# Stacked attention items: every transposition takes 128 rows, and columns of zeros are overwritten within the unit

## The chip, the cores and the metric

The kernel runs on one core of one Trainium2 chip. The metric is the device time of one execution in microseconds (us), the median of several runs. A run is also profiled once; the profile's span is the time from the first to the last instruction of the program on that core.

## The reference

Causal attention in blocks of 64 positions, then two dense stages. All data is float32.

```python
batch, n_heads, seq, head_dim = (4, 8, 576, 64)
scores = scale * np.matmul(q, k.transpose(0, 1, 3, 2))
mask = block_i >= block_j                    # blocks of 64
attn = softmax(where(mask, scores, -1e9))
x = np.matmul(attn, v)                       # as 2304 rows of 512
h = np.maximum(np.maximum(x @ w1, x @ w2), x @ w3);  x = h @ w_out     # 512 -> 768 -> 512
h = x @ w_in;  g = h * np.cos(h);  out = g @ moe2_w_out                # 512 -> 2048 -> 512
```

## The kernel before

Attention is cut into 32 items: batch (4), half of the rows (queries 0 to 319 and 320 to 575), pair of heads (4). An item goes through loads, `prep` (float32 split into two parts for the matrix products), `scores` (products into PSUM tiles SA and SB, row maximum on VectorE, exponential on ScalarE into the SBUF tiles `prob`, then each row is divided by its sum), `transposes` (TensorE turns 128 by 128 pieces of `prob` into the PSUM tile `tb`, and a copy by ScalarE or VectorE, `pt<-tb`, brings them to the SBUF tile `pt`), and `pv` (products of `pt` with the values, into the PSUM tile X). The matrix products of the first dense stage (tile `psm`) are put between the steps of the items as filling work; the second dense stage (`psm<-yh,w_in` and `po`) follows after the last item.

Items of batches 1 to 3 in the second half of the rows are "stacked" (line 572: `it.stacked = b > 0 and half == 1`); there are 3 x 4 = 12 of them. In a stacked item each 128-row tile of `prob` holds two blocks of 64 queries, and for each of its two heads (`e`) there are two tiles, a (448 columns used, `prob[6]` or `prob[7]`) and b (576 columns used, `prob[8]` or `prob[5]`). The causal mask makes the first 64 rows of a zero in its fourth piece of 128 columns (piece 3, counted from 0), and the first 64 rows of b zero in its fifth (piece 4). `transposes_stacked` therefore works in two units for each head. Unit h = 0 takes pieces 0 and 1 of a and b: four transpositions of 128 rows. Unit h = 1 takes piece 2 of a and b, piece 3 of a from row 64 on, piece 3 of b, and piece 4 of b from row 64 on: five transpositions, of which two take only the last 64 rows (written `64*128` in the profile: 64 rows, 128 columns loaded; the result has 64 columns). Both units fill one 512-column tile `tb`, which is then copied in one piece.

The order of all work is made by a planner (`Plan`). Calls to an engine are recorded as operations with a price and dependencies; those in a `with R.unit():` block are one operation. The planner then schedules all operations by list scheduling and emits the instructions of each engine in that order, so that each engine has a fixed queue. A transposition has a fixed price, whatever its size (`price`):

```python
if method == "transpose":
    return 109.0, late, False
```

For tiles in PSUM the planner takes the whole buffer as read or written, and for tiles in SBUF a range of columns of all rows. All calls pass through one helper line, so every instruction of the profile bears the same line number, L214, and is told apart by its tiles.

Of the kernel before, what the change touches and what calls it, by code (L numbers as in the profile page):

```python
# [19 lines left out]
P = 128  # L20
# [437 lines left out]
def fused_kernel(tc, qk, k1, v2, w1, w2, w3, wout, w_in2, w_out2, out):  # L458
# [11 lines left out]
    R = Plan(tc)  # L470
# [10 lines left out]
    ident = const.tile([P, P], F32, "ident")  # L481
# [191 lines left out]
    def transposes_stacked(it):  # L673
        it.pt = at.tile([P, 16 * P], F32, "pt", tag="pt")
        for e in range(2):
            a, b = (prob[where[e]] for *_, where in PAIRS)
            for h in range(2):
                tiles = [(a, 2 * h, 0), (b, 2 * h, 0)] + (
                    [(a, 1, 0), (b, 1, 0)] if h == 0 else [(a, 3, 64), (b, 3, 0), (b, 4, 64)])
                t = ps_x.tile([P, 512], F32, "tb", tag="T", bufs=2)  # L680
                with R.unit():
                    c0 = 0
                    for p, j, r in tiles:
                        R.tensor.transpose(t[:, c0:c0 + P - r], p[r:P, j * P:j * P + P], ident[r:P, r:P])
                        c0 += P - r
                c = 1024 * e + 512 * h
                R.copy(it.pt[:, c:c + 512], t)

# [57 lines left out]
    def transposes(it):  # L746
        if it.stacked:
            return transposes_stacked(it)
        order = it.f.order
        it.pt = at.tile([P, 16, P], F32, "pt", tag="pt")  # L750
        for c in range(0, len(order), 4):
            part = order[c:c + 4]
            n = P * len(part)
            t = ps_x.tile([P, 512], F32, "tb", tag="T", bufs=2)
            with R.unit():
                for x, (j, b) in enumerate(part):
                    R.tensor.transpose(t[:, x * P:x * P + P], prob[b][:, j * P:j * P + P], ident)
            R.copy(it.pt[:, c:c + len(part)].rearrange("p b n -> p (b n)"), t[:, :n])
# [349 lines left out]
```

## Time and profile before

| | us |
|---|---|
| runs: median of 3 (lowest, highest) | 893.09 (893.08, 893.38) |
| the profiled execution: its own time | 892.99 |
| the profiled execution: span of the core | 891.2 |
| TensorE matmul busy | 876.3 (98% of the span) |
| TensorE weight load busy | 720.7 (81%) |
| VectorE busy | 556.1 (62%) |
| ScalarE busy | 450.7 (51%) |

In the profile PE is a matmul and PEld the load of its weights, that is of the operand that stays in the array; for a transposition that is the piece of `prob`, and the identity streams past it. A matmul's duration includes its way through the array, so that the durations of neighbours overlap; what a matmul costs the queue is the distance from its start to the start of the next. DVE is VectorE, ACT is ScalarE, POOL is GpSimd, SP is SyncE. Between the span and the execution's own time lie 1.8 us.

### The profile page before, as it was taken

Reading aid. Unit: us, or ns where it says so; the run is one execution under the profiler, and the core shown is the slowest. Engines: PE = TensorE matmul, PEld = TensorE weight load, DVE = VectorE, ACT = ScalarE, POOL = GpSimd, SP = SyncE. Lnnn points to the kernel's source line nnn. Section 1 sums busy time; section 2 is a strip of 40 time slices with the busy share of each in tenths; the row PEclk is TensorE's granted clock in tenths of the full one; section 3 lists DMA queues with packets and bytes.
Section 4 is the critical chain, followed back from the end, with each engine's and each line's share of the span. In section 5 each row is a group of like instructions: output and inputs, shape, how many; then the busy total and the mean of one; then the engine's idle time right before and its main releaser. Section 6 shows DMA issues by size and latency. Waiting matters only on the chain.

```text
span 891.2 us, 12524 instructions
## 1 busy us (share of the span) xinstructions
PE 876.3 (98%) x4616; PEld 720.7 (81%) x4616; DVE 556.1 (62%) x1099; ACT 450.7 (51%) x974; POOL 6.5 (1%) x38
## 2 busy tenths in 40 slices
PE   7799999999999999999999999999999999999998
PEld 5577887888877888787789888888888888888897
DVE  6999987875566425534549797655464455455454
ACT  7997777775677515644555543332233223322333
POOL 0000000000000000000000000000000000000000
PEclk9999999999999999999999999999999999999999
DMA  7664637763346303511165851110001000100000
GB/s 258 227 206 148 187 119 232 246 192 120 94 140 232 113 1 125 201 61 54 64 205 180 331 190 48 48 48 1 0 25 48 1 0 1 48 1 0 24 24 24
DMA packets 43548, 95.05 MB, mean 107 GB/s; under 512 B 5856, under 2 KB 15072, under 8 KB 43488
## 3 DMA queue, kind: packets, MB, share of 16 engines
q1 hardware_dynamic: 43488, 94.26, 32.3%
q8 instruction: 36, 0.59, 0.3%
q14 instruction: 24, 0.20, 0.1%
HBM read 73.79 MB, written 20.45 MB: 106 GB/s over the span
## 4 chain that ended last, share of the span: by engine, by line
PE 95%; ACT 2%; DMA 1%; DVE 1%; issue 0%; SPq 0%; ACTq 0%; DVEq 0%
PE psm L214 56%; PE po L214 22%; PE tb L214 6%; PE X L214 5%; PE SA L214 3%; PE SB L214 3%; DMA raw<-w 1%; ACT prob L214 1%; ACT pt L214 0%; SPq L214 0%; DVE t L214 0%; DVE top L214 0%; ACT add L214 0%; DVE prob L214 0%; ACT t L214 0%
## 5 line engine op out<-in xcount | busy, mean ns | idle before, releaser
L214 PE MATMUL psm<-yh,w_in 128*128 128x512 f32 (+1 forms) x640 | 194.3, 368 | 0.0
L214 PE MATMUL po<-w_out,gh 128*128 128x512 f32 x576 | 177.6, 390 | 0.0
L214 ACT ACTIVATE th<-th,halfpi 128x512 f32<-128x512 f32 (+1 forms) x80 | 54.5, 682 | 189.1 <-DVE th L214 189.0
L214 PE MATMUL psm<-xhi,whi 128*128 128x512 f32 (+1 forms) x360 | 137.2, 381 | 0.0
L214 PEld LDWEIGHTS psm<-yh,w_in 128*128 128x128 f32 x640 | 117.0, 188 | 20.6
L214 PE MATMUL psm<-xlo,whi 128*128 128x512 f32 (+1 forms) x360 | 132.9, 369 | 0.0
L214 PE MATMUL psm<-xhi,wlo 128*128 128x512 f32 (+1 forms) x360 | 132.8, 369 | 0.0
L214 PEld LDWEIGHTS po<-w_out,gh 128*128 128x128 f32 x576 | 107.1, 188 | 21.2
L214 PE MATMUL psm<-yl,w_in 128*128 128x512 f32 (+1 forms) x320 | 117.7, 368 | 0.0
L214 PE MATMUL po<-w_out,gl 128*128 128x512 f32 x288 | 112.0, 389 | 0.0
L214 DVE TENSOR_SCALAR th<-psm 128x512 int32<-128x512 f32 (+1 forms) x80 | 50.9, 637 | 71.8 <-PE psm L214 71.7
L214 DVE TENSOR_TENSOR th<-psm,th 128x512 f32<-128x512 f32 (+1 forms) x80 | 50.9, 637 | 53.7 <-ACT th L214 53.7
L214 DVE TENSOR_TENSOR hm<-psm,hm 128x512 f32<-128x512 f32 (+1 forms) x60 | 38.1, 636 | 66.4 <-PE psm L214 65.6
L214 PEld LDWEIGHTS psm<-xhi,wlo 128*128 128x128 f32 x360 | 67.9, 189 | 11.8
L214 PEld LDWEIGHTS psm<-xhi,whi 128*128 128x128 f32 x360 | 67.9, 189 | 11.0
L214 PEld LDWEIGHTS psm<-xlo,whi 128*128 128x128 f32 x360 | 68.0, 189 | 9.1
L214 DVE TENSOR_TENSOR gl<-th,gh 128x512 fp32r<-128x512 f32 (+1 forms) x80 | 50.9, 636 | 38.3 <-ACT gh L214 38.3
L214 ACT CAST gh<-th 128x512 fp32r<-128x512 f32 (+1 forms) x76 | 43.9, 578 | 55.6 <-DVE th L214 55.6
L214 PE MATMUL tb<-ident,prob 128*128 128x128 f32 (+1 forms) x424 | 68.4, 278 | 3.4 <-ACT pt L214 2.9
L214 PEld LDWEIGHTS psm<-yl,w_in 128*128 128x128 f32 x320 | 60.3, 188 | 10.6
L214 ACT COPY pt<-tb 128x512 f32<-128x512 f32 (+1 forms) x101 | 55.9, 568 | 23.6 <-PE tb L214 23.1
L214 PEld LDWEIGHTS tb<-ident,prob 128*128 128x128 f32 (+1 forms) x424 | 51.1, 140 | 20.3 <-issue 5.2
(104 smaller groups left out, 1311.2 us busy)
## 6 DMA issues: line engine op xcount, KB each, us to landing
raw<-w SPq DMA_DIRECT2D x18, 512.0 KB, 3.8
raw<-w_in SPq DMA_DIRECT2D x16, 512.0 KB, 3.7
raw<-w_out SPq DMA_DIRECT2D x16, 512.0 KB, 3.9
k<-k SPq DMA_DIRECT2D x24, 288.0 KB, 3.0
vr<-v SPq DMA_DIRECT2D x16, 320.0 KB, 3.2
kept_in<-both SPq DMA_DIRECT2D x10, 512.0 KB, 3.6
w_in<-kept_in SPq DMA_DIRECT2D x10, 512.0 KB, 9.7
out<-osb SPq DMA_DIRECT2D x18, 256.0 KB, 2.0
```

What stands on the lines that cost most here:

```text
L214: return lambda: getattr(real, method)(*[value(a) for a in args], **{k: value(a) for k, a in kw.items()})
```

## The change

In `transposes_stacked`, each piece now gets the column `c0` of `tb` at which it is written, and every transposition takes all 128 rows and writes 128 columns. Unit h = 0 keeps its pieces, their order and places. In unit h = 1 the pieces that took 64 rows now write their 64 columns of zeros first, to columns that a later transposition of the unit fills: piece 3 of a is written to columns 192 to 319, then piece 2 of a to 0 to 127 and piece 2 of b to 128 to 255 (over the zeros in 192 to 255); piece 4 of b is written to 384 to 511, then piece 3 of b to 320 to 447 (over the zeros in 384 to 447). What stands in `tb` at the end of the unit, and so the copy and all that follows, is as it was.

```diff
-                tiles = [(a, 2 * h, 0), (b, 2 * h, 0)] + (
-                    [(a, 1, 0), (b, 1, 0)] if h == 0 else [(a, 3, 64), (b, 3, 0), (b, 4, 64)])
+                tiles = [(a, 0, 0), (b, 0, P), (a, 1, 2 * P), (b, 1, 3 * P)] if h == 0 else [
+                    (a, 3, 192), (a, 2, 0), (b, 2, P), (b, 4, 384), (b, 3, 320)]
                 t = ps_x.tile([P, 512], F32, "tb", tag="T", bufs=2)
                 with R.unit():
-                    c0 = 0
-                    for p, j, r in tiles:
-                        R.tensor.transpose(t[:, c0:c0 + P - r], p[r:P, j * P:j * P + P], ident[r:P, r:P])
-                        c0 += P - r
+                    for p, j, c0 in tiles:
+                        R.tensor.transpose(t[:, c0:c0 + P], p[:, j * P:j * P + P], ident)
                 c = 1024 * e + 512 * h
                 R.copy(it.pt[:, c:c + 512], t)
```

## Rows read from the trace of the kernel before

**Rows 1.** First lines of the page: busy us (share of span) xinstructions.

```profile
span 891.2 us, 12524 instructions
PE 876.3 (98%) x4616; PEld 720.7 (81%) x4616; DVE 556.1 (62%) x1099; ACT 450.7 (51%) x974; POOL 6.5 (1%) x38
```

**Rows 2.** Busy time by stretch: length, engines' busy us (instructions), clock, DMA share, GB/s.

```profile
100.00:451.00 351.00, 351.00 (x1952) 281.98 (x1951) 207.15 (x428) 213.09 (x498) 5.08 (x24) 1.00 0.43 137
451.00:891.00 440.00, 436.58 (x2151) 370.74 (x2149) 258.74 (x445) 153.81 (x259) 0.00 (x0) 1.00 0.18 60
```

**Rows 3.** Waits of PE, 0 to 100 us, first and last: us, times, longest.

```profile
PE SB L214 <- ACT prob L214: 4.1, 4, 1.1
...
PE SB L214 <- ACT knat L214: 0.3, 1, 0.3
```

**Rows 4.** Groups by form, PE, 128 to 442: xcount | busy us, mean ns | idle.

```profile
L214 PE MATMUL tb<-ident,prob 128*128 128x128 f32 x240 | 39.7, 280 | 0.0
L214 PE MATMUL tb<-ident,prob 64*128 64x64 f32 x48 | 13.0, 271 | 0.0
```

**Rows 5.** Timeline of PE, both units: start, length, instruction (first of several merged).

```profile
253.88 0.39 PE L214 MATMUL psm<-hl,vhi 128*128 128x512 f32 x1
254.10 0.39 PE L214 MATMUL psm<-hh,vlo 128*128 128x512 f32 x1
254.34 0.60 PE L214 MATMUL tb<-ident,prob 128*128 128x128 f32 x4
...
255.71 1.05 PE L214 MATMUL tb<-ident,prob 128*128 128x128 f32 x5
256.68 0.50 PE L214 MATMUL psm<-hh,vhi 128*128 128x512 f32 x1
257.02 0.39 PE L214 MATMUL psm<-hl,vhi 128*128 128x512 f32 x1
```

**Rows 6.** Timeline of the weight loads, same unit of five.

```profile
255.58 0.27 PEld L214 LDWEIGHTS tb<-ident,prob 128*128 128x128 f32 x2
256.01 0.60 PEld L214 LDWEIGHTS tb<-ident,prob 64*128 64x128 f32 x3 [0.17 <-issue]
256.68 0.19 PEld L214 LDWEIGHTS psm<-hh,vhi 128*128 128x128 f32 x1
```

**Rows 7.** Timeline of PE where all transpositions have 128 rows.

```profile
217.15 0.60 PE L214 MATMUL tb<-ident,prob 128*128 128x128 f32 x4
...
217.81 0.40 PE L214 MATMUL psm<-xlo,whi 128*128 128x512 f32 x1
...
286.92 0.71 PE L214 MATMUL tb<-ident,prob 128*128 128x128 f32 x5
287.38 0.36 PE L214 MATMUL SA<-kh,qh 128*128 128x256 f32 x1
...
329.31 1.03 PE L214 MATMUL tb<-ident,prob 128*128 128x128 f32 x8
...
330.41 0.39 PE L214 MATMUL psm<-xlo,whi 128*128 128x512 f32 x1
```

**Rows 8.** Timeline of the weight loads of those eight.

```profile
329.07 1.03 PEld L214 LDWEIGHTS tb<-ident,prob 128*128 128x128 f32 x8
```

**Rows 9.** Timeline of PE: a run of nine (unit of four, then unit of five).

```profile
236.28 1.48 PE L214 MATMUL tb<-ident,prob 128*128 128x128 f32 x9
...
238.02 0.39 PE L214 MATMUL psm<-xlo,whi 128*128 128x512 f32 x1
```

**Rows 10.** Timeline of PE with scores (SA) as the neighbours.

```profile
373.14 0.60 PE L214 MATMUL tb<-ident,prob 128*128 128x128 f32 x4
...
373.70 0.29 PE L214 MATMUL SA<-kl,ql 128*128 128x288 f32 x1
373.84 1.05 PE L214 MATMUL tb<-ident,prob 128*128 128x128 f32 x5
...
375.05 0.29 PE L214 MATMUL SA<-kl,ql 128*128 128x288 f32 x1
```

**Rows 11.** Busy time, stretches with changed units: PE, PEld, DVE, ACT, POOL.

```profile
128.00:180.00 52.00, 52.00 (x326) 40.61 (x325) 39.85 (x86) 38.94 (x94) 0.00 (x0) 1.00 0.68 222
236.00:281.00 45.00, 45.00 (x273) 34.87 (x273) 27.52 (x55) 33.31 (x81) 0.00 (x0) 1.00 0.49 157
370.00:442.00 72.00, 72.00 (x379) 57.02 (x379) 31.53 (x56) 36.56 (x75) 0.00 (x0) 1.00 0.18 56
```

**Rows 12.** Timeline of DVE: last scaling of `prob` before a transposition.

```profile
249.66 0.51 DVE L214 TENSOR_SCALAR prob<-prob,sums 128x576 f32<-128x576 f32 x1
```

**Rows 13.** Timeline of PE at that place.

```profile
250.69 0.55 PE L214 MATMUL tb<-ident,prob 128*128 128x128 f32 x3
```

**Rows 14.** Waits of ACT and DVE, 128 to 180, longest totals: us, times, longest.

```profile
ACT pt L214 <- PE tb L214: 4.9, 8, 1.7
DVE top L214 <- PE SB L214: 5.6, 7, 1.6
DVE top L214 <- PE SA L214: 2.7, 3, 1.7
```

**Rows 15.** Timeline of ACT: copy after the unit of four of rows 5.

```profile
254.97 0.59 ACT L214 COPY pt<-tb 128x512 f32<-128x512 f32 x1 [1.12 <-PE tb L214]
```

## The prediction

> **What bounds the kernel now.** The page's busy line comes first: PE has 98% of the span, no other engine over 62% [rows 1]. An average does not say that PE sets the pace where the change is, so the table by stretch comes next: from 100 to 451 us PE is busy for all 351.00 of 351.00 us, at a granted clock of 1.00, while DVE and ACT are busy for 207 and 213 [rows 2]. Since busy PE time includes the way through the array, it alone does not rule out short waits, and the list of PE's waits is third: the stretch up to 100 us has seven rows, 11.2 us together, and the list of the whole span has the same seven, so none lies behind [rows 3]. The 48 transpositions of 64 rows all start between 128 and 442 us, with no idle PE time before any of them [rows 4]. So all that changes lies in a stretch where PE issues without a pause, and what a unit of transpositions gives up there goes to the end of the span one for one, unless another engine becomes late. Behind 451 us there are 2151 matmuls of PE, 436.58 us in 440.00, which also only follow earlier [rows 2].
>
> **What a unit costs now.** A matmul's length overlaps its neighbours, so a unit is read from starts: from its first transposition to the start of the second matmul behind it, since the first matmul behind it starts early and stays long (at 256.68 it lasts 0.50 us, its like 0.39 [rows 5]). A unit of five before `psm`: 255.71 to 257.02, 1.31 us [rows 5]. The same measure where all transpositions have 128 rows: four take 217.15 to 217.81, 0.66 us; eight take 329.31 to 330.41, 1.10 us [rows 7]. Four more cost 0.44, so one costs 0.11 us, and a unit of five would take 0.66 + 0.11 = 0.77. The excess of today's unit is 1.31 - 0.77 = 0.54 us. A run of nine (a unit of four, then one of five) confirms it: 236.28 to 238.02 is 1.74 us [rows 9], against 1.10 + 0.11 = 1.21, an excess of 0.53. With scores as the neighbours: 373.84 to 375.05 is 1.21, the unit of four ahead of it 373.14 to 373.70 is 0.56, plus 0.11 gives 0.67, an excess of 0.54 [rows 10]. It does not depend on what follows.
>
> Where the excess sits is seen in the weight loads. Eight loads of 128 rows run from 329.07 for 1.03 us without a gap, beside the matmuls, which start at 329.31 [rows 7, 8]: each load is done under the matmul ahead. In the unit of five the third load, the first of 64 rows, waits 0.17 us for nothing that the profile shows ("issue"), and the next matmul's load starts only at 256.68, with that matmul [rows 6]. I read this as the array running empty each time the height of the operand changes, four times in a unit: into and out of each of the two 64-row pieces.
>
> **The change part by part.** Removed: 48 transpositions of 64 rows, two in each of 12 items x 2 heads = 24 units [rows 4], and with them the four changes of height in each unit. Added: 48 transpositions of 128 rows in their place; five stay five. Each is twice as high and writes twice the columns. No row shows one that overwrites another's columns, so I bound it: below, nothing beyond the 0.11 us that a full transposition costs [rows 7]; above, by the wait in the third rival. I take the lower end, since the nearest row shows overwriting in flight: the `psm` matmuls of one group write the same 512 columns, start 0.22 us apart (253.88, 254.10) and last 0.39, so the second starts to write while the first is still under way, with no gap [rows 5]. Sum for a unit: 1.31 - 0.77, or 1.74 - 1.21; I take 0.53. 24 x 0.53 = 12.7 us.
>
> Moved: only the order inside units of h = 1. The first transposition there now reads the fourth piece of a. That calls for no later operation than before: one scaling instruction covers all used columns of a tile (128x576 in [rows 12]), and the unit h = 0 ahead of it already reads the same tiles. The planner's price of a transposition is 109 ns in either size, the recorded operations and the column ranges that it sees are the same, so I expect the same queues on every engine; no DMA is added or passed. Unit h = 0 issues the same instructions as before. The copy `pt<-tb` stays one of 512 columns, 0.59 us [rows 15]; it ends earlier with its unit.
>
> What could be late next: scaling of `prob`, which must end before the first transposition. At 250.69 it had ended at 249.66 + 0.51 = 250.17, 0.52 us earlier [rows 12, 13], and between that item's last scores and this place stands no changed unit, so both move together. Where a changed unit does lie between, PE arrives 0.53 us earlier and uses up such a margin, and might stand for a few tenths. I take nothing off for it in the forecast.
>
> Against the profiled execution: span 891.2 - 12.7 = 878.5, its own time 892.99 - 12.7 = 880.3. The median of the runs stands 0.10 above that execution: 893.09 - 12.7 = 880.4.
>
> **Rivals.** First, part of the gain is absorbed. Between 128 and 180 us lie 8 of the 24 units (16 transpositions of 64 rows), and DVE and ACT are busy for 39.85 and 38.94 of 52 us [rows 11]. If their chain set the pace there as soon as PE is faster, the 8 x 0.53 = 4.2 us of that stretch would be lost: 884.6. Against it: in that stretch ACT waits 4.9 us for `tb` and DVE 8.3 us for scores [rows 14], which an earlier PE gives back; from 236 to 281 and from 370 to 442, with 8 units each, the two engines have more room [rows 11]. 0.15, most of it for a loss of 1 to 2 us.
>
> Second, the change doesn't do what it says: the excess comes not from the height but from the place of those pieces, and stays. 893.1. Against it: the unit of five at 286.92, of 128 rows throughout, takes 0.46 us to the next matmul [rows 7], today's 0.97 [rows 5]. 0.03.
>
> Third, the other side: the overwriting transposition waits until the zeros under it are written. In a unit, piece 2 of b comes two transpositions (0.22 us) after piece 3 of a, and piece 3 of b one (0.11) after piece 4 of b. A transposition lasts 0.27 us [rows 4], a handover 0.03 (`tb` ends at 254.34 + 0.60 = 254.94, ACT starts at 254.97 [rows 5, 15]). If only the matmul waits, the two lose 0.30 - 0.22 = 0.08 and 0.30 - 0.11 = 0.19, together 0.27 of the 0.53: 893.09 - 24 x 0.26 = 886.9. If the wait also keeps back the weight load (0.27 for two, about 0.14 each [rows 6]), they lose 0.55: 24 x 0.02 slower, 893.6; and if each such wait also costs the 0.17 us of idle time that the height change shows [rows 6], 0.89: 24 x 0.36 = 8.6 slower, 901.7. It decides from 0.265 us for each overwriting transposition. Against it stands the row of `psm` above, and that one engine's queue is in order. 0.02 for 886.9, 0.03 for the slower end.
>
> Fourth, a mechanism of the weight loads: full-height loads wait for the matmul ahead, since both use the whole array, and only pieces of another height get in beside it. Each transposition of 128 rows would then cost 0.27 + 0.14 = 0.41 us, a unit of five 2.05 instead of 1.31: 24 x 0.74 = 17.8 slower, 910.9. The Trainium skill says so in TensorE: Matmul & The Clock Gate, Part 3 (What overlaps and what doesn't): a weight load runs beside a matmul only when their row groups differ. By that rule one would keep the 64-row pieces. The trace says otherwise: the eight full-height loads follow each other under running matmuls [rows 7, 8], and it is the 64-row load that stands [rows 6]. 0.01.
>
> **How the numbers follow.** Forecast 0.76: 880.4, by itself 879.6 (a unit saves 0.56, 0.02 of reading error in each) to 882. The range reaches to the whole price of the first rival, 884.6. Left out are 886.9 and beyond, 0.09 together. What a measurement of this kernel can tell from no change is about 0.2%, 1.8 us. Faster: 0.76 + 0.15 + 0.02 = 0.93; the same: 0.03; slower: 0.03 + 0.01 = 0.04.
>
> **What would show it.** In the changed kernel's profile: no form `64*128` under `tb`, 424 transpositions of 128 rows in all and 4616 matmuls; units of five that take 0.77 us to the second matmul before `psm`, runs of nine 1.21; weight loads in them without idle time by "issue"; PE's list of waits still empty behind 100 us. A gain below 12 us with units at 0.77 means new waits of PE, by name in that list, and points to the first rival; units near 1.04 or 1.31 and more point to overwriting (third) or to the place of the pieces (second). A changed order of the queues would make the argument from the planner wrong.

## The result, and the profile after

| | before | after |
|---|---|---|
| median of 4 runs (lowest, highest), us | 893.09 (893.02, 893.38) | 881.27 (880.12, 882.92) |
| ratio, 95% interval | | 0.9868 [0.9851, 0.9886] |
| the profiled execution: its own time; span | 892.99; 891.2 | 880.12; 878.3 |

The kernel became 11.8 us faster by the medians, 12.9 by the two profiled executions. The forecast was 880.4.

The first lines of the page after, as in [rows 1]:

```profile
span 878.3 us, 12524 instructions
PE 863.8 (98%) x4616; PEld 718.1 (82%) x4616; DVE 555.7 (63%) x1099; ACT 449.6 (51%) x974; POOL 6.5 (1%) x38
```

The number of instructions is the same on every engine, and in the traces every engine issues them in the same order, by their tiles, as the prediction expected of the planner. PE's busy time fell by 12.5 us; DVE and ACT have done the same work.

The forms under `tb`, on PE between 127 and 430 us (columns as in [rows 4]):

```profile
L214 PE MATMUL tb<-ident,prob 128*128 128x128 f32 x288 | 39.6, 274 | 0.0
```

240 + 48 = 288: the 64-row form is gone, the number is kept. Two units of the changed kernel on PE's timeline, four then five, answering [rows 5], the loads of the second, answering [rows 6], and a run of nine, answering [rows 9]:

```profile
248.28 0.60 PE L214 MATMUL tb<-ident,prob 128*128 128x128 f32 x4
...
249.66 0.71 PE L214 MATMUL tb<-ident,prob 128*128 128x128 f32 x5
250.12 0.48 PE L214 MATMUL psm<-hh,vhi 128*128 128x512 f32 x1
250.44 0.39 PE L214 MATMUL psm<-hl,vhi 128*128 128x512 f32 x1
```

```profile
249.53 0.60 PEld L214 LDWEIGHTS tb<-ident,prob 128*128 128x128 f32 x5
250.09 0.19 PEld L214 LDWEIGHTS psm<-hh,vhi 128*128 128x128 f32 x1
```

```profile
231.76 1.14 PE L214 MATMUL tb<-ident,prob 128*128 128x128 f32 x9
232.66 0.47 PE L214 MATMUL psm<-xhi,whi 128*128 128x512 f32 x1
232.98 0.39 PE L214 MATMUL psm<-xlo,whi 128*128 128x512 f32 x1
```

The five loads follow one another for 0.60 us with no idle time marked, and the load of the next matmul starts at 250.09, 0.03 before that matmul; the unit of [rows 6] had 0.17 of "issue" and behind it a load that started with its matmul. The unit of five takes 249.66 to 250.44, 0.78 us, where [rows 5] had 1.31. The run of nine (the last fence) takes 231.76 to 232.98, 1.22, where [rows 9] had 1.74.

PE's waits after, whole span, complete (the list between 100 and 450 us is empty):

```profile
PE SB L214 <- ACT prob L214: 4.1, 4, 1.1
PE tb L214 <- ACT pt L214: 2.5, 4, 0.9
PE psm L214 <- POOL ident L214: 1.4, 1, 1.4
PE SA L214 <- ACT prob L214: 1.0, 1, 1.0
PE X L214 <- ACT pt L214: 0.9, 1, 0.9
PE tb L214 <- DVE prob L214: 0.4, 1, 0.4
PE SB L214 <- ACT knat L214: 0.3, 1, 0.3
```

No wait has come up in place of what was removed. For the sum, one stretch is measured in every kernel: from a unit of four transpositions some 4 us ahead of the first changed unit to the first `po` matmul, the start of the last stage's output products. All 24 units lie in it, and the early part of the kernel lies outside. Before, then after:

```profile
124.58 0.66 PE L214 MATMUL tb<-ident,prob 128*128 128x128 f32 x4
...
505.05 0.39 PE L214 MATMUL po<-w_out,gh 128*128 128x512 f32 x1
```

```profile
124.24 0.66 PE L214 MATMUL tb<-ident,prob 128*128 128x128 f32 x4
...
492.16 0.39 PE L214 MATMUL po<-w_out,gh 128*128 128x512 f32 x1
```

380.47 against 367.92: 12.55 us were saved in the stretch, of 12.9 in the span. Another 0.34 had come about ahead of it (124.58 to 124.24), where the two kernels issue the same instructions; that part differs from one execution to the next (the same place starts at 124.74 in a second profile of the changed kernel, below), and is not the change's doing. Behind the stretch nothing changed: 891.2 - 505.05 = 386.2 and 878.3 - 492.16 = 386.1.

### The profile page after: what moved, and what is told of

Same layout as the page of the kernel before. It is cut to its first block, busy times and chain, and to the rows that moved or that the text cites. A ratio compares the mean times of both kernels' runs of the same rounds, so it can differ in the third digit from the quotient of the medians.

```text
span 878.3 us, 12524 instructions
## 1 busy us (share of the span) xinstructions
PE 863.8 (98%) x4616; PEld 718.1 (82%) x4616; DVE 555.7 (63%) x1099; ACT 449.6 (51%) x974; POOL 6.5 (1%) x38
## 4 chain that ended last, share of the span: by engine, by line
PE 95%; DVE 2%; ACT 1%; DMA 1%; issue 0%; POOL 0%; SPq 0%; POOLq 0%
PE psm L214 57%; PE po L214 22%; PE X L214 5%; PE tb L214 5%; PE SA L214 3%; PE SB L214 3%; DMA raw<-w 1%; ACT prob L214 1%; DVE t L214 1%; DVE top L214 1%; ACT pt L214 0%; DVE prob L214 0%; DVE wlo L214 0%; DVE xlo L214 0%; DVE ql L214 0%
## 5 line engine op out<-in xcount | busy, mean ns | idle before, releaser
L214 PEld LDWEIGHTS psm<-xhi,wlo 128*128 128x128 f32 x360 | 67.9, 189 | 11.8
L214 ACT COPY pt<-tb 128x512 f32<-128x512 f32 (+1 forms) x101 | 55.4, 568 | 17.3 <-PE tb L214 16.6
L214 PE MATMUL tb<-ident,prob 128*128 128x128 f32 x424 | 60.4, 275 | 3.0 <-ACT pt L214 2.5
L214 PEld LDWEIGHTS po<-w_out,gl 128*128 128x128 f32 x288 | 54.1, 188 | 11.3
```

Source lines behind the costliest of these rows:

```text
L214: return lambda: getattr(real, method)(*[value(a) for a in args], **{k: value(a) for k, a in kw.items()})
```

## The experiments

All times stand beside runs of the kernel before on the same chip as the experiment. The mean granted clock differs from run to run, so times are compared at a mean clock of 0.999 or more, and where there is only one run, by the stretch from the trace.

**One head alone.** The kernel before, with the new order and height where `h and e == 0`:

```diff
+                if h and e == 0:
+                    tiles = [(a, 3, 192), (a, 2, 0), (b, 2, P), (b, 4, 384), (b, 3, 320)]
...
+                        if h and e == 0:
+                            R.tensor.transpose(t[:, r:r + P], p[:, j * P:j * P + P], ident)
+                            continue
```

> The change in unit h = 1 of the first head of an item (e = 0) alone, 12 of the 24 units. Theory (each unit's 0.53 us goes to the end of the span one for one): 12 x 0.53 = 6.4 us less, 886.7; the changed units take 0.77, the others 1.31. Rival (the gain of the denser units around 128 to 180 us is partly absorbed by ACT and DVE): two doses that don't add up, this one nearer to the whole change, 885 or less.

Measured: median 887.58 (886.50 to 889.15) against 895.15 for before, ratio 0.9910 [0.9885, 0.9935]; at clocks of 0.999 it took 886.50 and 886.99, before at 1.000 took 892.47 and 892.79. That is 5.9 us by their means, and by the trace:

```profile
127.04 0.66 PE L214 MATMUL tb<-ident,prob 128*128 128x128 f32 x4
...
236.64 1.14 PE L214 MATMUL tb<-ident,prob 128*128 128x128 f32 x9
237.54 0.47 PE L214 MATMUL psm<-xhi,whi 128*128 128x512 f32 x1
237.86 0.39 PE L214 MATMUL psm<-xlo,whi 128*128 128x512 f32 x1
...
244.05 1.48 PE L214 MATMUL tb<-ident,prob 128*128 128x128 f32 x9
245.46 0.50 PE L214 MATMUL psm<-xhi,whi 128*128 128x512 f32 x1
245.80 0.40 PE L214 MATMUL psm<-xlo,whi 128*128 128x512 f32 x1
...
501.20 0.39 PE L214 MATMUL po<-w_out,gh 128*128 128x512 f32 x1
```

Within one execution the changed run of nine takes 1.22 and the unchanged one 1.75. The stretch is 501.20 - 127.04 = 374.16: 6.31 us less than before for 12 units, 0.526 each, and twice that is 12.62, where all 24 gave 12.55. The doses add up: half of the units gave half of the gain, within 0.1 us, and PE's list of waits is empty behind 100 us here too. So the rival is out.

**The two 64-row pieces next to each other.** The same transpositions as in the kernel before, in another order:

```diff
...
-                    [(a, 1, 0), (b, 1, 0)] if h == 0 else [(a, 3, 64), (b, 3, 0), (b, 4, 64)])
...
+                    (a, 2, 0, 0), (b, 2, 0, P), (a, 3, 64, 256), (b, 4, 64, 448), (b, 3, 0, 320)]
...
```

An entry is tile, piece, first row, first column in `tb`.

> Unit h = 1 keeps the two 64-row pieces and their 64 columns, but in the order a2, b2, a3 (64 rows), b4 (64 rows), b3, each to the columns it has in the kernel before: two changes of height in a unit instead of four, the same instructions. Theory (a change of height costs): about half of the excess goes, a unit of five takes 1.02 to 1.06 us instead of 1.31 to the second matmul behind it, 24 units save 6 to 7 us: 886 to 887. Rival (each 64-row transposition is dear in itself): the unit stays at 1.31 and the time at 893.1.

Measured: median 886.01 (884.52 to 887.59), ratio 0.9897 [0.9873, 0.9921]; at a clock of 1.000 it took 884.52 and 885.05, before 892.47 and 892.79: 7.8 us less (7.86 by the stretch, in the table below). The loads and the run of nine, on the timelines of PEld and PE:

```profile
232.81 0.81 PEld L214 LDWEIGHTS tb<-ident,prob 128*128 128x128 f32 x6
233.79 0.40 PEld L214 LDWEIGHTS tb<-ident,prob 64*128 64x128 f32 x3 [0.17 <-issue]
```

```profile
233.05 1.34 PE L214 MATMUL tb<-ident,prob 128*128 128x128 f32 x9
234.15 0.48 PE L214 MATMUL psm<-xhi,whi 128*128 128x512 f32 x1
234.46 0.39 PE L214 MATMUL psm<-xlo,whi 128*128 128x512 f32 x1
```

The 0.17 us of "issue" still stands ahead of the first 64-row load, but the three loads from there on take 0.40 together, where [rows 6] had 0.60 for its three. Nine take 1.41, 0.20 over the 1.21 of 128 rows, where four changes of height cost 0.53. With the same instructions, rows and columns, 0.33 x 24 = 7.9 us go away by order alone. So the price hangs on the change of height and not on a 64-row transposition as such. The expected half was 0.25 to 0.29; it was 0.20, so two changes cost less than half of four, and the saving was larger than the 6 to 7 us expected.

The starts inside the two runs of nine show it directly (each line comes from a narrow window of the timeline, so that nothing earlier is merged into it). First the kernel before, from its first 64-row piece on, then `adjacent`, its two 64-row pieces:

```profile
237.03 0.27 PE L214 MATMUL tb<-ident,prob 64*128 64x64 f32 x1
237.23 0.33 PE L214 MATMUL tb<-ident,prob 128*128 128x128 f32 x1
237.49 0.27 PE L214 MATMUL tb<-ident,prob 64*128 64x64 f32 x1
```

```profile
233.80 0.27 PE L214 MATMUL tb<-ident,prob 64*128 64x64 f32 x1
233.91 0.48 PE L214 MATMUL tb<-ident,prob 64*128 64x64 f32 x2
```

Where the height changes, the next transposition starts 0.20 and 0.26 us later (237.03, 237.23, 237.49); a 64-row piece behind a 64-row piece starts 0.11 later (233.80, 233.91), as one of 128 rows does behind its like [rows 7].

With the height two other things change: a 64-row transposition streams 64 columns in place of 128, and its rows lie in the lower half of the tile. The first alone is not what costs: in the kernel before, score products of full height go from 128 to 64 columns without such a gap:

```profile
287.99 0.27 PE L214 MATMUL SA<-kh,ql 128*128 128x128 f32 x1
288.10 0.24 PE L214 MATMUL SA<-kh,qh 128*128 128x64 f32 x1
288.18 0.28 PE L214 MATMUL SA<-kl,qh 128*128 128x64 f32 x1
```

The distances are 0.11 and 0.08 us. The second was not tested: every 64-row piece takes rows 64 to 127, so the number of rows and their place are not told apart.

**What a change costs by its place.** Three more orders, one run each, all with the two 64-row pieces of the kernel before; the lists give tile and piece, and 64 where a piece starts at row 64:

```text
two_last:  (a, 2), (b, 2), (b, 3), (a, 3, 64), (b, 4, 64)
ends:      (a, 3, 64), (a, 2), (b, 2), (b, 3), (b, 4, 64)
alternate: (a, 2), (a, 3, 64), (b, 2), (b, 4, 64), (b, 3)
```

> Order a2, b2, b3, a3 (64 rows), b4 (64 rows) in unit h = 1: two changes of height as in the kernel adjacent, but the way back to 128 rows is to the next work (psm or scores) instead of to a transposition. Theory A (only the number of changes counts): excess 0.20 us for a unit, as adjacent showed, nine transpositions before psm 1.41. Theory B (each change is priced by its neighbours: into 64 rows 0.09, back to a transposition 0.10, back to psm 0.19): excess 0.09 + 0.19 = 0.28 to 0.29, nine take 1.50.

> Order a3 (64 rows), a2, b2, b3, b4 (64 rows): four changes, the two 64-row pieces far apart. Theory A (the number of changes): excess 0.53 as in the kernel before, nine take 1.74. Theory B (by neighbours): 0.09 + 0.09 for a3, 0.09 + 0.19 for b4, together 0.47; nine take 1.69.

> Order a2, a3 (64 rows), b2, b4 (64 rows), b3: four changes with one full transposition between the two 64-row pieces, as in the kernel before, but the last change goes back to a transposition. Theory A: excess 0.53, nine take 1.74. Theory B: 0.09 + 0.09, then into 64 rows behind a single full transposition 0.15, then 0.10 back: 0.43 to 0.44; nine take 1.65.

Their runs of nine on PE's timeline, in this order:

```profile
234.94 1.19 PE L214 MATMUL tb<-ident,prob 128*128 128x128 f32 x9
...
236.40 0.40 PE L214 MATMUL psm<-xlo,whi 128*128 128x512 f32 x1
```

```profile
237.07 1.48 PE L214 MATMUL tb<-ident,prob 128*128 128x128 f32 x9
...
238.82 0.40 PE L214 MATMUL psm<-xlo,whi 128*128 128x512 f32 x1
```

```profile
236.71 1.63 PE L214 MATMUL tb<-ident,prob 128*128 128x128 f32 x9
...
238.41 0.40 PE L214 MATMUL psm<-xlo,whi 128*128 128x512 f32 x1
```

1.46, 1.75 and 1.70 us, so excesses of 0.25, 0.54 and 0.49 over 1.21. The stretch of the trace, which holds all 24 units, gives nearly the same for each kernel; the last column is what it has over the changed kernel's 367.92, divided by 24:

| kernel | starts, us | stretch, us | changes of height in a unit | excess of a unit, us |
|---|---|---|---|---|
| before | 124.58, 505.05 | 380.47 | 4 | 0.52 |
| `ends` | 125.38, 505.81 | 380.43 | 4 | 0.52 |
| `alternate` | 125.26, 505.02 | 379.76 | 4 | 0.49 |
| `two_last` | 125.59, 499.15 | 373.56 | 2 | 0.24 |
| `adjacent` | 123.95, 496.56 | 372.61 | 2 | 0.20 |

Two changes of height cost 0.20 to 0.25, four 0.49 to 0.54. Neither theory hits all three orders. Theory B, a sum of prices set by the neighbours, is out by 0.03 to 0.07 at each of them in the runs of nine (0.28 to 0.29, 0.47 and 0.43 to 0.44 expected); theory A, the number of changes, is out by 0.04 to 0.05 at two and by 0.01 at the third. So the number of changes sets the price in the main; the place adds or takes some 0.04 us for a unit, and no simple sum was found for that. The three runs took 887.14, 893.78 and 892.98 us beside one run of the kernel before at 897.11; they differ in mean clock, so the units and not these times are compared.

**The changed kernel again.**

> The changed kernel once more. With the granted clock at 1.00 all through, 880.1 as in its profiled execution. Theory (the scatter of 880.1 to 882.9 is the granted clock, 0.996 to 1.000 in its runs, and not waits): runs again between 880 and 883, longer where the mean clock is lower, about 0.9 us for 0.001. Rival (a wait that some executions have): longer runs at a clock of 1.000.

Measured: 880.00 to 884.58, median 883.37 of five, against 895.15 of before (892.47 to 897.00, nine runs), ratio 0.9856 [0.9832, 0.9880]. The mean clock of each run orders them:

| mean granted clock | before, us | changed kernel, us |
|---|---|---|
| 0.999 to 1.000 | 892.47, 892.79 | 880.00, 880.56 |
| 0.998 | 893.83 | |
| 0.995 to 0.996 | 894.76, 895.15, 895.27 | 883.37, 883.37 |
| 0.993 to 0.994 | 896.59, 896.96, 897.00 | 884.58 |

By the means of its rows, the two kernels differ by 11.7 to 12.4 at like clocks. The longest run lies above the 883 that was expected, and the time grew by some 0.7 us for each 0.001 of clock, not 0.9; no long run had a clock near 1.000, as the rival would want. The stretch from the trace is 492.61 - 124.74 = 367.87, as in the first profile within 0.05. Where the clock falls is seen in the profiles of the experiments, stretch 10 to 20 us; the changed kernel's first profile, then the kernel `one_head`, with its second such place:

```profile
10.00:20.00 10.00, 6.94 (x45) 4.71 (x43) 10.00 (x33) 9.96 (x30) 0.00 (x0) 1.00 0.86 292
```

```profile
10.00:20.00 10.00, 7.90 (x43) 5.75 (x41) 8.88 (x30) 9.07 (x26) 0.00 (x0) 0.83 0.74 247
40.00:50.00 10.00, 7.97 (x42) 4.89 (x43) 7.46 (x19) 7.93 (x18) 0.00 (x0) 0.83 0.52 166
```

A mean of 0.83 says that a part of such a stretch ran at the lower level, 1.2 GHz: from 15.70 to 18.80 us `one_head` had 0.52, the changed kernel 1.00. What it costs stands in the rows there: the ten score products from 15.54 to the transpositions at 18.77 took 3.23 us in `one_head`, their like 1.79 in the changed kernel (15.69 to 17.48). Those places lie in the first 50 us, where PE has waits of up to 1.5 us, some 75 us ahead of the first changed unit. The changed kernel's own longer runs have no trace, so that their clock fell at the same place is likely but not shown. The four runs of the first table fit: the changed kernel's 880.12, 881.18, 881.37 and 882.92 had mean clocks of 1.000, 0.998, 0.998 and 0.996.

## Why the prediction was right

The time lay inside the range, 0.9 us over the forecast, and the mechanism was the one described. Step by step:

- **The bound.** Right: PE issues without a wait behind 100 us before and after, and what the units gave up reached the end one for one (12.55 us in the stretch, 386 us behind it unchanged).
- **The unit.** 0.77 us was worked out for a unit of five and 0.78 measured; 1.21 for nine and 1.22 measured. The saving of a unit was put at 0.53 and came out at 12.55 / 24 = 0.52. Of the 0.2 us between 12.7 and 12.55 I did not find a single place; an error of 0.01 in the reading of a unit would make it up. That the profiled executions differ by 12.9, as near to 12.7, is in part luck: 0.34 of it came about ahead of the changed units.
- **The cause.** That the change of height costs, and not the 64-row piece, is shown by the order alone: the same pieces with two changes cost 0.20 to 0.25 us where four cost 0.49 to 0.54. That the array runs empty at a change is still only a reading of the idle weight loads; what the runs show is the price and that it follows the number of changes. The TensorEngine Tiling (Array Packing) page of the Trainium skill, under Tiling Modes, Key Properties, says that a change of tiling mode drains the engine. These traces agree in so far as each change has its price, 0.10 to 0.13 us on average; they don't show the drain itself.
- **Overwritten columns cost nothing that can be seen.** The five transpositions with two overwrites run from 249.66 to the next matmul at 250.12, 0.46 us, as the five at 286.92 without any in [rows 7], to 287.38. The third rival is out.
- **No new wait.** The first rival did not come: PE's list is empty behind 100 us, ACT's waits for `tb` fell from 23.1 to 16.6 us in the whole span, and one head gave half of what two gave.
- **The fourth rival**, full-height loads that wait for the matmul ahead, is contradicted again: five such loads in 0.60 us, beside matmuls that start from 249.66 on. The Trainium skill, TensorE: Matmul & The Clock Gate, Part 3 (What overlaps and what doesn't), lets a weight load overlap a running matmul only where their row groups differ; the traces of before and after show full-height loads under full-height matmuls, and the measurement decides.
- **The 0.9 us.** Against the profiled execution, the forecast was 880.3 and 880.12 was measured. The clock was the same in both where PE works: before's mean of 0.999 comes from the end of its span, where no matmul is left (last fence of this section: from 890.10 us on no engine is busy, at a granted clock of 0.56). Of the four runs behind the median, three had a mean clock of 0.996 to 0.998. The sum had no term for a scatter of the clock, and it took the 0.10 by which the median had stood above the profiled execution as a constant; here it was 1.15.

```profile
890.10:891.20 1.10, 0.00 (x0) 0.00 (x0) 0.00 (x0) 0.00 (x0) 0.00 (x0) 0.56 0.00 0
```

## What to carry to other kernels

On an engine that never waits, read what an instruction costs from start to start, including the first instructions behind the group, and compare with the nearest group without the suspect form: here 96 changes of the operand's height, 0.13 us each on average, were 1.4% of the kernel though no view lists them as a wait of PE. In this kernel the smaller operands were dearer than full ones because they stood among full ones; padding them to full height cost nothing beyond a full transposition, and putting the two small ones side by side alone gave back 0.28 to 0.33 of the 0.53 us. A spread of single runs is best taken apart by one stretch of the trace that holds all the changed work.

## What was not expected of the hardware

- Of two 64-row pieces side by side, the second starts 0.11 us behind the first, as one of 128 rows does behind its like; two changes of height cost 0.20 to 0.25 us whether the way back is to a transposition or to `psm`.
- A like delay stands elsewhere in the kernel, also after the change, at the products X of the `pv` step, which load 128 rows but 64 columns (`128*64`). In the kernel before, `psm` follows `psm` after 0.23 us and X follows `psm` after 0.31:

```profile
260.46 0.39 PE L214 MATMUL psm<-hl,vhi 128*128 128x512 f32 x1
260.69 0.39 PE L214 MATMUL psm<-hh,vlo 128*128 128x512 f32 x1
261.00 1.30 PE L214 MATMUL X<-pt,vr 128*64 128x256 f32 x10
```

  No wait of PE is listed there. Whether it is the same price, paid for a change in the loaded columns, was not tested.
- The granted clock fell to the 1.2 GHz level for part of the first 50 us in the profiled executions of four of the experiments' kernels. Runs at a mean clock of 0.994 took 4.2 us longer than runs at 1.000 (896.85 against 892.63, means of three and of two runs of the kernel before). What sets a fall off stays open: `one_head` and the changed kernel issue the same instructions in those 50 us, and of their profiles only that of `one_head` shows a fall.
